# Half-width products for the super-tiles that carry only one layer

## The chip, the cores and the metric

The kernel runs on one core of one Trainium2 chip. The metric is the device time of one execution in microseconds (us), on that core. Every run below is of the state "fast" (none was over 1.5% above the fastest of its kernel). Engines are called PE (TensorE, matmul), PEld (its weight loads), DVE (VectorE), ACT (ScalarE), POOL (GpSimd) and SP (DMA issue).

## The reference, cut to what matters

```python
def _A_ref(x, mem0, Wq, Wk, Wv, Wo, seg_len):      # S=2048, Dm=448, H=16, Dh=256, M=8, seg_len=32
    mem = mem0
    for s in range(n_seg):                          # 64 segments, one after the other
        h = concatenate([mem, xs], axis=1)          # 8 memory rows + 32 tokens
        q, k, v = h @ Wq, h @ Wk, h @ Wv
        p = softmax(where(mask, q @ k * scale, -1e9))
        o = (p @ v) @ Wo
        mem = o[:, :M, :]                           # the memory rows feed the next segment
        outs.append(o[:, M:, :])

def _B_ref(x, W_gate, W_up, W_down):                # F=1792
    gate = relu-like(x @ W_gate);  return (gate * (x @ W_up)) @ W_down

x = x + _A_ref(layernorm(x), ...);  x = x + _B_ref(layernorm(x), ...)   # layer 0
x = x + _A_ref(layernorm(x), ...);  x = x + _B_ref(layernorm(x), ...)   # layer 1, same weights
```

The memory makes a recurrence over the 64 segments in each layer. Layer 1 can start segment s as soon as layer 0 has finished it.

## The kernel before

The two layers run as a pipeline, layer 1 four segments behind layer 0 (`LAG = 4`). One *step* t handles segment t of layer 0 and segment t-4 of layer 1; there are 68 steps. Two steps make a *super-tile* p (34 of them) of 128 rows: 64 tokens of layer 0 in rows 0 to 63 and 64 tokens of layer 1 in rows 64 to 127. Super-tiles 0 and 1 hold only layer 0, super-tiles 32 and 33 only layer 1; half of their rows are empty.

In each step the recurrence goes: score products of the segment (224 matmuls in `t_unit`), scores of the memory rows, softmax, transposes, the memory's value products, and the *memory value-sum* `un_mem` (56 products with 32 weight columns, four at once). Its result feeds the scores of the next step. Off this recurrence, but on TensorE too, lie the value-sum of the tokens (`un`), the layer norm (`ln_b`) and the gated MLP (`b_layer`), which run as filler while the recurrence waits for DVE and ACT. Their result is the input of layer 1 four steps later.

```python
    def un(self, p):                                        # value-sum: 56 products, 448 columns each
        for k in range(0, NO, 2):
            S.mm(lambda k=k: [MM(S.bO[:, 0:D], S.U[:, o, :], S.N[:, o, :], start=(o == 0), stop=(o == NO - 1)) for o in (k, k + 1)],
                 2 * S.pitch(D), uk[k // 16], S.ps(4))
        S.dve(lambda E: E.tensor_tensor(S.XB[:, p % 2, :], S.bO[:, 0:D], S.XA[:, p % 4, :], ALU.add), D, ...)

    def b_layer(self, p):
        for k in range(7):                                  # gate and up: 112 products, 128 columns each
            ...MM(R[w].b()[:, i * 128:i * 128 + 128], W[:, kt, fc * 128:fc * 128 + 128], S.xBT[:, kt, :], ...)
            S.act(... Relu ...);  S.dve(... tensor_tensor(hB, gT, up, ALU.mult) ...)
        for k in range(7):                                  # down: 14 products, 448 columns each
            S.mm(lambda k=k: [MM(S.bO[:, 0:D], S.hB[:, fc, :], S.Wd[:, fc, :], ...) for fc in (2 * k, 2 * k + 1)], ...)
        # then XA (input of layer 1, super-tile p + 2) and ys (output) = bO + XB
```

A scheduler in the file (`_Order`) sorts all these operations before the program is written: a greedy list scheduling by the longest path to the end. A change in one place can therefore reorder instructions elsewhere.

## Time and profile before

| | before |
|---|---|
| time | 1806.25 us median of 3 (1805.87 to 1811.62) |
| PE busy | 1733.2 of 1807.4 us (96%) |
| DVE, ACT busy | 59%, 40% |
| PE in the chain that ended last | 88% |
| one cycle of four steps in the middle | 103.09 us |

These lines are from the page of the profiled execution: the span, the busy time of each engine with its share and the number of instructions, and the shares of the chain of work that ended last.

```profile
span 1807.4 us, 67812 instructions
...
PE 1733.2 (96%) x30612; PEld 1247.2 (69%) x30612; DVE 1074.6 (59%) x3057; ACT 726.8 (40%) x2048; POOL 90.5 (5%) x155
...
PE 88%; DVE 7%; ACT 2%; SPq 1%; issue 1%; DMA 0%; DVEq 0%
```

PE is the limit. Its busy time is modelled, however, so the argument rests on the *starts* of matmuls in the trace. They give the pitch of a product: 189 ns for 448 columns, 56 ns for 128, 25 ns for 40.

The groups of instructions by line, engine and shape show the three kinds of product that the change touches (columns: engine, operation, output<-inputs, weight rows*columns, rows x columns of the moving operand, count | busy us, mean ns of one | idle before).

```profile
L127 PE MATMUL b<-Nw,big 128*128 128x448 bf16 x1928 | 414.7, 357 | 7.2 <-DVE big L683 5.2 <-issue 0.6
L127 PE MATMUL b<-xBT,big 128*128 128x128 bf16 x3808 | 233.5, 220 | 0.8 <-ACT xBT L682 0.7
...
L127 PE MATMUL b<-big,hB 128*128 128x448 bf16 x476 | 112.8, 354 | 0.0
```

The value-sum (`Nw,big`: 34 x 56 = 1904 products, the other 24 belong to the setup), gate/up (`xBT,big`, 34 x 112) and down (`big,hB`, 34 x 14) have one shape each: the four half-empty super-tiles pay the full width.

The end of the kernel is serial. The timeline of its last 28 us (start, duration, engine, line, operation, count, and the idle time before with what ended it):

```profile
1779.00 10.77 PE L127 MATMUL b<-Nw,big 128*128 128x448 bf16 x56
1789.81 0.62 DVE L953 TENSOR_TENSOR XB<-b,XA 128x448 bf16<-128x448 f32 x1 [10.10 <-PE b L127]
...
1792.64 0.40 PE L127 MATMUL b<-ident,xn 128*128 128x128 bf16 x4 [2.87 <-DVE xn L719]
...
1793.73 7.06 PE L127 MATMUL b<-xBT,big 128*128 128x128 bf16 x96 [0.69 <-ACT xBT L682]
...
1804.37 0.63 DVE L980 TENSOR_TENSOR ys<-b,XB 64x448 bf16<-64x448 f32 x1 [1.36 <-PE b L127]
```

The value-sum of super-tile 33 takes 10.8 us, the layer norm leaves PE waiting for 2.9 us and then 0.7 us, and gate, up and down take 10.6 us more.

These are stretches of the span with the busy time of each engine and the granted clock of PE (columns: stretch, length, busy us of PE, PEld, DVE, ACT, POOL with counts, PEclk, DMA share, GB/s): steps 1 to 5, steps 6 to 61, steps 62 to 65, and step 66 to the end.

```profile
93.54:211.18 117.64, 115.83 (x2095) 82.11 (x2095) 65.85 (x212) 37.80 (x108) 4.68 (x9) 0.98 0.01 3
211.18:1660.17 1448.99, 1407.34 (x25258) 1027.20 (x25257) 873.82 (x2436) 588.88 (x1652) 62.54 (x112) 1.00 0.02 5
1660.17:1754.57 94.40, 92.97 (x1750) 65.98 (x1749) 49.86 (x167) 38.26 (x113) 4.47 (x8) 1.00 0.02 4
1754.57:1807.39 52.82, 45.37 (x665) 32.49 (x664) 20.66 (x61) 13.58 (x39) 0.00 (x0) 0.97 0.02 4
```

The granted clock (the share of PE's full clock that the trace shows it was given) is not quite 1.00 at the two ends. The trace lists where: stretches of 3.4 us (once 6.8 us) at exactly half clock, at 36, 80 and 90 us, four times in the middle (at 503, 814, 1125 and 1435 us), and at 1793.5 us, in the gate/up products of the tail.

### The profile page before, as it was taken

To read this page: it belongs to the slowest core of one execution; us is meant where nothing else is said; L and a number is where in the kernel's file an instruction comes from. 1 tells how busy PE (TensorE), PEld (TensorE's weight loads), DVE (VectorE), ACT (ScalarE), POOL (GpSimd) and SP (SyncE) were. 2 spreads that over 40 slices of the span, in tenths; PEclk is the share of its full clock that TensorE was granted. 3 is DMA by queue.
4 is the path that set the end of the run, shared out by engine and by line. 5 is a ranking of instruction groups with operands and counts; after the bars stand their busy time and mean duration, and the time that the engine had idled before them with its cause. 6 is when DMAs were issued, how large, how long until landed. Compare 5 with 4: busy or idle time off the path is not lost.

```text
span 1807.4 us, 67812 instructions
## 1 busy us (share of the span) xinstructions
PE 1733.2 (96%) x30612; PEld 1247.2 (69%) x30612; DVE 1074.6 (59%) x3057; ACT 726.8 (40%) x2048; POOL 90.5 (5%) x155
## 2 busy tenths in 40 slices
PE   6899999999999999999999999999999999999998
PEld 2567667767766677677766776776667767766666
DVE  7645566665656566565655655565666656565553
ACT  5433433444343344434343444334334443434432
POOL 3000000000000000000000000000000000000000
PEclk9999999999999999999999999999999999999999
DMA  9700000000000000000000000000000000000000
GB/s 228 212 4 4 3 5 4 5 5 5 4 5 5 3 5 5 5 4 5 5 5 4 5 5 5 4 5 5 5 4 5 5 5 3 4 4 4 4 4 4
DMA packets 55760, 27.52 MB, mean 15 GB/s; under 512 B 44584, under 2 KB 54576, under 8 KB 55472
## 3 DMA queue, kind: packets, MB, share of 16 engines
q1 hardware_dynamic: 55120, 22.94, 5.2%
q8 instruction: 241, 3.95, 0.9%
q14 instruction: 47, 0.39, 0.1%
q10 hardware_dynamic: 352, 0.24, 0.1%
HBM read 10.33 MB, written 1.84 MB: 7 GB/s over the span
## 4 chain that ended last, share of the span: by engine, by line
PE 88%; DVE 7%; ACT 2%; SPq 1%; issue 1%; DMA 0%; DVEq 0%
PE b L127 88%; ACT big L682 2%; SPq L518 1%; DVE stat L712 1%; DVE big L683 1%; DVE TTs L683 1%; ACT hT L682 1%; DVE XB L953 1%; DVE xn L719 1%; DVE ys L980 1%; DVE XA L976 0%; DMA Nw<-in_A_Wq_dram 0%; DVE Es L841 0%; DVE stat L840 0%; DVE TTm L683 0%
## 5 line engine op out<-in xcount | busy, mean ns | idle before, releaser
L127 PEld LDWEIGHTS b<-hT,Mw 128*128 128x128 bf16 x15232 | 538.3, 100 | 26.3 <-DVE hT L683 12.0
L127 PE MATMUL b<-hT,Mw 128*128 128x80 bf16 (+1 forms) x15232 | 544.9, 199 | 5.7 <-DVE hT L683 3.9
L127 PE MATMUL b<-Nw,big 128*128 128x448 bf16 (+1 forms) x1936 | 415.8, 357 | 7.2 <-DVE big L683 5.2
L683 DVE CAST TTs<-b 128x320 bf16<-128x320 f32 (+5 forms) x572 | 261.2, 457 | 87.0 <-PE b L127 86.1
L127 PEld LDWEIGHTS b<-Nw,big 128*128 128x128 bf16 (+1 forms) x1936 | 172.2, 99 | 167.8 <-issue 22.3
L127 PE MATMUL b<-xBT,big 128*128 128x128 bf16 x3808 | 233.5, 220 | 0.8 <-ACT xBT L682 0.7
L127 PEld LDWEIGHTS b<-xBT,big 128*128 128x128 bf16 x3808 | 216.7, 98 | 3.2 <-ACT xBT L682 0.9
L683 DVE CAST TTm<-b 128x80 bf16<-128x80 f32 (+5 forms) x575 | 133.6, 232 | 125.9 <-PE b L127 95.0
L127 PE MATMUL b<-Nw,UTm 128*32 128x448 bf16 x3752 | 191.5, 355 | 0.6 <-ACT UTm L682 0.6
L683 DVE CAST big<-b 128x512 bf16<-128x512 f32 (+1 forms) x192 | 122.8, 661 | 104.4 <-PE b L127 103.4
L682 ACT ACTIVATE big<-b 128x512 bf16<-128x512 f32 (+1 forms) x320 | 152.6, 525 | 55.2 <-PE b L127 52.0
L127 PEld LDWEIGHTS b<-Nw,UTm 128*32 128x32 bf16 x3752 | 95.1, 97 | 88.7 <-issue 19.8
L683 POOL COPY hK<-xn 32x448 bf16<-32x448 bf16 x136 | 75.9, 558 | 1526.8 <-DVE xn L719 1520.5
L968 ACT ACTIVATE gT<-b 128x256 bf16<-128x256 f32 x238 | 91.5, 384 | 144.4 <-PE b L127 140.3
L682 ACT ACTIVATE TTs<-b 64x256 bf16<-64x256 f32 (+5 forms) x312 | 128.5, 412 | 31.2 <-PE b L127 26.6
L969 DVE TENSOR_TENSOR hB<-gT,b 128x256 bf16<-128x256 bf16 x238 | 99.5, 418 | 69.7 <-ACT gT L968 60.1
L682 ACT ACTIVATE TTm<-b 64x64 bf16<-64x64 f32 (+5 forms) x309 | 70.5, 228 | 143.4 <-PE b L127 136.8
L895 DVE TENSOR_TENSOR lo<-b,hi 128x448 bf16<-128x448 f32 x67 | 41.6, 620 | 127.3 <-ACT hi L894 127.3
L894 ACT ACTIVATE hi<-b 128x448 bf16<-128x448 f32 x67 | 36.5, 544 | 193.5 <-PE b L127 193.5
L127 PE MATMUL b<-big,hB 128*128 128x448 bf16 x476 | 112.8, 354 | 0.0
L682 ACT ACTIVATE hK<-b 8x448 bf16<-8x448 f32 x94 | 50.4, 536 | 124.3 <-PE b L127 122.9
L127 PE MATMUL b<-PTs,hK 40*128 40x512 bf16 (+1 forms) x640 | 86.7, 348 | 13.5 <-DVE XA L976 7.6
(96 smaller groups left out, 1392.5 us busy)
## 6 DMA issues: line engine op xcount, KB each, us to landing
big<-in_A_Wo_dram SPq DMA_DIRECT2D x3, 896.0 KB, 5.6
out_dram<-ys SPq DMA_DIRECT2D x32, 56.0 KB, 1.9
big<-in_B_W_down_dram SPq DMA_DIRECT2D x1, 1568.0 KB, 7.2
XA<-in_A_x_dram SPq DMA_DIRECT2D x28, 56.0 KB, 2.1
big<-in_B_W_up_dram SPq DMA_DIRECT2D x1, 1344.0 KB, 7.8
big<-in_B_W_gate_dram SPq DMA_DIRECT2D x1, 1344.0 KB, 8.8
Nw<-in_A_Wo_dram SPq DMA_DIRECT2D x1, 896.0 KB, 6.2
XA<-in_A_x_dram ACTq DMA_DIRECT2D x4, 56.0 KB, 4.3
```

Source lines behind the costliest of these rows:

```text
L127: ins = E.matmul(out, lhsT=lhsT, rhs=rhs, **kw)
L518: S.q.add("dma", ("sp",), {"sp": 3600.0}, lambda E: E.dma_start_transpose(out=st[w, q], in_=src[w][:, q * 1024:(q + 1) * 1024]), (), [(w, ...
L682: return E.activation(out(), src(), ACT.Copy)
L683: return E.tensor_copy(out(), src())
L712: S.dve(lambda E: E.bn_stats(st[:, so:so + 6], x), D, rd, [(key, 0)])
L719: S.dve(lambda E, a=a, b=b, src=src: E.tensor_scalar(S.xn[:, i, a:b], src, st[:, so + 6:so + 7], st[:, so + 8:so + 9], op0=ALU.subtract, o ...
L894: S.act(lambda E: E.activation(S.hi[:, :], b[:, 0:D], ACT.Copy), D, S.ps(6), [("hi",)])
L895: S.dve(lambda E: E.tensor_tensor(S.lo[:, :], b[:, 0:D], S.hi[:, :], ALU.subtract), D, S.ps(6) + [("hi",)], [("lo",)])
L953: S.dve(lambda E: E.tensor_tensor(S.XB[:, p % 2, :], S.bO[:, 0:D], S.XA[:, p % 4, :], ALU.add), D, S.ps(4) + [("XA", p % 4, 0), ("XA", p % ...
L968: S.act(lambda E, k=k, R=R: E.activation(S.gT[:, k % 2, 0:256], R[0].b()[:, 0:256], ACT.Relu), 256, R[0].res(), [("gT", k % 2)])
L969: S.dve(lambda E, k=k, R=R: E.tensor_tensor(S.hB[:, 2 * k:2 * k + 2, :].rearrange("p a b -> p (a b)"), S.gT[:, k % 2, 0:256], R[1].b()[:, ...
L980: S.dve(lambda E: E.tensor_tensor(S.ys[64:128, p % 2, :], S.bO[64:128, 0:D], S.XB[64:128, p % 2, :], ALU.add), D, S.ps(4, half=(1,)) + [(" ...
```

## The change

The intent: in the four super-tiles with one active layer, use the 64 rows that exist. The value-sum and down products then have only 64 weight columns, so two of them fit into the array side by side, one in each column half, each summing every second chunk; two adds on DVE join the two sums. Gate and up move 64 columns instead of 128.

```diff
+    def rows(p):
+        return slice(0, 64) if p < LAG // 2 else slice(64, 128) if p >= NSEG // 2 else slice(0, 128)
+    def halves(self, dst, base, base_keys, r, keys):
+        S.dve(lambda E: E.tensor_tensor(S.part[r, :], S.bO[0:64, 0:D], base, ALU.add), ...)
+        S.dve(lambda E: E.tensor_tensor(dst, S.bO[64:128, 0:D], S.part[r, :], ALU.add), ...)
     def un(self, p):
+        r = S.rows(p)
+        if r.stop - r.start == 128: ...as before...
+        else:
+            for k in range(0, NO, 4):
+                S.mm(lambda k=k: [MM(S.bO[64 * (o % 2):64 * (o % 2) + 64, 0:D], S.U[:, o, r], S.N[:, o, :], start=(o < 2), stop=(o >= NO - 2))
+                                  for o in range(k, k + 4)], 2 * S.pitch(D), uk[k // 16], S.ps(4), mode=6)
+            S.halves(S.XB[r, p % 2, :], S.XA[r, p % 4, :], ...)
     def b_layer(self, p):
-            fcs = (2 * k, 2 * k + 1)                        # two chunks of 128 columns a bank
+        w = r.stop - r.start;  m = 256 // w                 # or four of 64
...
-                return [MM(R[w].b()[:, i * 128:i * 128 + 128], ..., S.xBT[:, kt, :], ...)
+                return [MM(R[x].b()[:, i * w:i * w + w], ..., S.xBT[:, kt, r], ...)
...
-            S.mm(lambda k=k: [MM(S.bO[:, 0:D], S.hB[:, fc, :], S.Wd[:, fc, :], ...) for fc in (2 * k, 2 * k + 1)], ...)
+            S.mm(lambda k=k: [MM(S.bO[:, 0:D] if full else S.bO[64 * (fc % 2):64 * (fc % 2) + 64, 0:D], S.hB[:, fc, 0:w], ...)
+                              for fc in (2 * k, 2 * k + 1)], (2 if full else 1) * S.pitch(D), ..., mode=0 if full else 6)
```

(Cut: the joining adds of `b_layer`, a memset of the unused half of `XB`, and the `part` buffer.)

More of the change, by code (lines that the diff above doesn't have):

```diff
@@ L427, in alloc @@
         self.stat = self.sb("stat", [128, 96], F32)
+        self.part = self.sb("part", [128, D], F32)
         self.cvec = self.sb("cvec", [128, 2], F32)
@@ L559, in setup @@
         S.pool(lambda E: E.memset(S.Pm[:, :], 0.0), 128, (), [("Pm",)])
+        S.pool(lambda E: E.memset(S.XB[64:128, :, :], 0.0), 900, (), [("XB", 0), ("XB", 1)])
         S.pool(lambda E: E.memset(S.Ps[:, :, :], 0.0), 512, (), [("Ps",)])
@@ L945, in u_seg @@
                      R[l].res(), [("U", s, l, c)])
+    @staticmethod
+    def rows(p):
+        return slice(0, 64) if p < LAG // 2 else slice(64, 128) if p >= NSEG // 2 else slice(0, 128)
+    def halves(self, dst, base, base_keys, r, keys):
+        S = self
+        S.dve(lambda E: E.tensor_tensor(S.part[r, :], S.bO[0:64, 0:D], base, ALU.add), D, S.ps(4, half=(0,)) + base_keys, [("part",)])
+        S.dve(lambda E: E.tensor_tensor(dst, S.bO[64:128, 0:D], S.part[r, :], ALU.add), D, S.ps(4, half=(1,)) + [("part",)], keys)
     def un(self, p):
         S = self
+        r = S.rows(p)
         uk = [[("U", s, l, c) for s in range(2) for l in range(2)] for c in range(4)]
-        for k in range(0, NO, 2):
-            S.mm(lambda k=k: [MM(S.bO[:, 0:D], S.U[:, o, :], S.N[:, o, :], start=(o == 0), stop=(o == NO - 1)) for o in (k, k + 1)],
-                 2 * S.pitch(D), uk[k // 16], S.ps(4))
-        S.dve(lambda E: E.tensor_tensor(S.XB[:, p % 2, :], S.bO[:, 0:D], S.XA[:, p % 4, :], ALU.add), D,
-              S.ps(4) + [("XA", p % 4, 0), ("XA", p % 4, 1)], [("XB", p % 2)])
+        if r.stop - r.start == 128:
+            for k in range(0, NO, 2):
+                S.mm(lambda k=k: [MM(S.bO[:, 0:D], S.U[:, o, :], S.N[:, o, :], start=(o == 0), stop=(o == NO - 1)) for o in (k, k + 1)],
+                     2 * S.pitch(D), uk[k // 16], S.ps(4))
+            S.dve(lambda E: E.tensor_tensor(S.XB[:, p % 2, :], S.bO[:, 0:D], S.XA[:, p % 4, :], ALU.add), D,
+                  S.ps(4) + [("XA", p % 4, 0), ("XA", p % 4, 1)], [("XB", p % 2)])
+        else:
+            for k in range(0, NO, 4):
+                S.mm(lambda k=k: [MM(S.bO[64 * (o % 2):64 * (o % 2) + 64, 0:D], S.U[:, o, r], S.N[:, o, :], start=(o < 2), stop=(o >= NO - 2))
+                                  for o in range(k, k + 4)], 2 * S.pitch(D), uk[k // 16], S.ps(4), mode=6)
+            S.halves(S.XB[r, p % 2, :], S.XA[r, p % 4, :], [("XA", p % 4, r.start // 64)], r, [("XB", p % 2)])
         S.load_x(p + 4)
@@ L958, in b_layer @@
         S = self
-        for k in range(7):
-            fcs = (2 * k, 2 * k + 1)
-            R = [S.tile("R", 1) for w in range(2)]
-            def mms(fcs=fcs, R=R):
-                return [MM(R[w].b()[:, i * 128:i * 128 + 128], W[:, kt, fc * 128:fc * 128 + 128], S.xBT[:, kt, :], start=(kt == 0), stop=(kt == 3))
-                        for w, W in ((0, S.Wg), (1, S.Wu)) for i, fc in enumerate(fcs) for kt in range(4)]
-            S.mm(mms, 16 * S.pitch(128), [("xBT",)] + [(nm, x) for nm in ("Wg", "Wu") for x in "abz"], R[0].res() + R[1].res() + [("hB", k)])
-            S.act(lambda E, k=k, R=R: E.activation(S.gT[:, k % 2, 0:256], R[0].b()[:, 0:256], ACT.Relu), 256, R[0].res(), [("gT", k % 2)])
-            S.dve(lambda E, k=k, R=R: E.tensor_tensor(S.hB[:, 2 * k:2 * k + 2, :].rearrange("p a b -> p (a b)"), S.gT[:, k % 2, 0:256],
-                                                      R[1].b()[:, 0:256], ALU.mult), 256, R[1].res() + [("gT", k % 2)], [("hB", k)])
@@ L971, in b_layer, with mms @@
-        for k in range(7):
-            S.mm(lambda k=k: [MM(S.bO[:, 0:D], S.hB[:, fc, :], S.Wd[:, fc, :], start=(fc == 0), stop=(fc == NFC - 1)) for fc in (2 * k, 2 * k + 1)],
-                 2 * S.pitch(D), [("hB", k), ("Wd",)], S.ps(4))
+        r = S.rows(p)
+        w = r.stop - r.start
+        m = 256 // w
+        for k in range(-(-NFC // m)):
+            fcs = range(m * k, min(m * k + m, NFC))
+            n = len(fcs) * w
+            R = [S.tile("R", 1) for _ in range(2)]
+            hk = [("hB", f // 2) for f in fcs[::2]]
+            def mms(fcs=fcs, R=R):
+                return [MM(R[x].b()[:, i * w:i * w + w], W[:, kt, fc * 128:fc * 128 + 128], S.xBT[:, kt, r], start=(kt == 0), stop=(kt == 3))
+                        for x, W in ((0, S.Wg), (1, S.Wu)) for i, fc in enumerate(fcs) for kt in range(4)]
+            S.mm(mms, 8 * len(fcs) * S.pitch(w), [("xBT",)] + [(nm, x) for nm in ("Wg", "Wu") for x in "abz"],
+                 R[0].res() + R[1].res() + hk)
+            S.act(lambda E, k=k, R=R, n=n: E.activation(S.gT[:, k % 2, 0:n], R[0].b()[:, 0:n], ACT.Relu), n, R[0].res(), [("gT", k % 2)])
+            S.dve(lambda E, k=k, R=R, n=n, fcs=fcs: E.tensor_tensor(
+                S.hB[:, fcs[0]:fcs[-1] + 1, 0:w], S.gT[:, k % 2, 0:n].rearrange("p (a b) -> p a b", b=w),
+                R[1].b()[:, 0:n].rearrange("p (a b) -> p a b", b=w), ALU.mult), n, R[1].res() + [("gT", k % 2)], hk)
@@ L974, in b_layer @@
+        full = w == 128
+        for k in range(7):
+            S.mm(lambda k=k: [MM(S.bO[:, 0:D] if full else S.bO[64 * (fc % 2):64 * (fc % 2) + 64, 0:D], S.hB[:, fc, 0:w], S.Wd[:, fc, :],
+                                 start=(fc < (1 if full else 2)), stop=(fc >= NFC - (1 if full else 2))) for fc in (2 * k, 2 * k + 1)],
+                 (2 if full else 1) * S.pitch(D), [("hB", k), ("Wd",)], S.ps(4), mode=0 if full else 6)
+        xb = [("XB", p % 2)]
         if p < NSEG // 2:
             q = p + LAG // 2
-            S.dve(lambda E: E.tensor_tensor(S.XA[64:128, q % 4, :], S.bO[0:64, 0:D], S.XB[0:64, p % 2, :], ALU.add), D,
-                  S.ps(4, half=(0,)) + [("XB", p % 2)], [("XA", q % 4, 1)])
+            if full:
+                S.dve(lambda E: E.tensor_tensor(S.XA[64:128, q % 4, :], S.bO[0:64, 0:D], S.XB[0:64, p % 2, :], ALU.add), D,
+                      S.ps(4, half=(0,)) + xb, [("XA", q % 4, 1)])
+            else:
+                S.halves(S.XA[64:128, q % 4, :], S.XB[0:64, p % 2, :], xb, r, [("XA", q % 4, 1)])
@@ L978, in b_layer @@
         if p >= LAG // 2:
             q = p - LAG // 2
-            S.dve(lambda E: E.tensor_tensor(S.ys[64:128, p % 2, :], S.bO[64:128, 0:D], S.XB[64:128, p % 2, :], ALU.add), D,
-                  S.ps(4, half=(1,)) + [("XB", p % 2)], [("ys", p % 2)])
+            if full:
+                S.dve(lambda E: E.tensor_tensor(S.ys[64:128, p % 2, :], S.bO[64:128, 0:D], S.XB[64:128, p % 2, :], ALU.add), D,
+                      S.ps(4, half=(1,)) + xb, [("ys", p % 2)])
+            else:
+                S.halves(S.ys[64:128, p % 2, :], S.XB[64:128, p % 2, :], xb, r, [("ys", p % 2)])
```

## The prediction

> **What bounds it now.** TensorE. On the page PE is busy 1733.2 of 1807.4 us (96%) and the chain of waits is 88% PE. VectorE is 59% busy. The stretches between two memory value-sums (one per step, timeline) repeat in a cycle of four steps: 25.7, 25.65, 26.9, 24.8 us, each within 0.8 to 1.8 us of its matmul work (pitch times count). The two first and two last super-tiles carry one layer but pay full width in their value-sum (56 matmuls N=448), gate/up (112, N=128) and down (14, N=448) products.
>
> **Costs.** From matmul starts in the trace: 448 columns 189 ns, 128 columns 56 ns, 40 columns 25 ns. The Trainium skill, "TensorE: Matmul & The Clock Gate", Back-to-back issue gap, gives N/2.4 + 2.5 ns with a floor of about 25 ns; the trace agrees, so I estimate 29 ns at N=64. Two column-half products of 448 columns already run in the setup (weights folded, 64-column outputs): the two start 3 ns apart and pairs follow every 189 ns, so halves really are two for one. A switch of tiling costs: first product after it 85 to 96 ns late, the next pair 210 instead of 189, and 96 ns on leaving. ("TensorEngine Tiling (Array Packing)", Key Properties: a mode switch drains; the trace shows it.) About 0.2 us per excursion.
>
> Per super-tile: value-sum 10.6 to 5.3 us, gate/up 6.3 to 3.3, down 2.65 to 1.3: 9.6 us, 38 us for four. The instruction order of the new kernel leaves steps 6 to 61 with the same matmuls; it adds about 30 tiling switches, some 3 us. One more VectorE add of 448 columns (0.63 us) per value-sum and per down product. The Pool memset is off the chain.
>
> **How much counts** (estimates, step by step):
> - Steps 1 to 5: now 20.5, 22.8, 23.6, 25.7, 25.1 us. Matmul work falls by 3.6, 5.9, 2.0, 5.7, 1.8. Steps 1 and 2 then hit the recurrence (memory value-sum, hi, lo, transposes, 224 score products, softmax, transposes, copy: about 17 us for one layer), switches take some: net about -16.
> - Steps 62 to 65: work falls by 5.3, but in the new order the last full down product moves behind the memory value-sum, and the next layer norm and score products wait for it, so about -2.5.
> - Step 67 with super-tile 32's GLU: -4.
> - Tail, all serial, 1779.0 to 1805.0: value-sum -5.3, gate/up -3.0, down -1.2, two extra adds +1.3: -8.
>
> Sum about -30 us: 1776 us, 1.7% less. Just under the 2% line, because four of 34 super-tiles change and about a fifth of the 38 us is given back to switches, extra adds and the recurrence.
>
> **Range** 1768 to 1785. Faster by over 2% 0.15, same 0.84, slower 0.01.
>
> **What would show it.** The timeline: column-half pairs at 189 ns, N=64 at about 29 ns, tail from the last value-sum's start to the end about 18 us instead of 26; steps 1 to 5 together about 101 us instead of 118; the four-step cycle still 103.1 us; more VectorE and fewer PE shares in the chain at the ends.
>
> **What would make it wrong.** Column-half weight loads not hidden (pair pitch over 189 ns); N=64 held by its weight loads; the recurrence longer than 17 us, or hidden so well that nearly all 38 us are gained; other half-clock windows: the clock now halves for 3.4 us about every 310 us, costing 1.4 us each, and their number may change by one or two, above all in the tail, where PE waits through the layer norm.

## More of the kernel before

The experiments ran in four rounds on four chips, with the kernel before run again in each: its 34 executions there lay between 1805.2 and 1812.1 us (0.4%), its medians between 1807.6 and 1808.4. So a few microseconds out of 1800 can be told apart with several runs, and differences of one or two between kernels of different rounds can't.

## The result

The changed kernel took 1783.91 us (median of 4, 1782.1 to 1784.83), the kernel before 1807.05 us in the same rounds. The ratio is 0.9866, 95% interval 0.9847 to 0.9885. (Ratios here are the mean time of one kernel's fast runs over that of the other's of the same rounds, so not quite the ratio of the medians quoted beside them.) That is 1.3% faster, within 2%. The forecast was 1776 us and 1.7%; the range 1768 to 1785 holds the result, near its upper edge.

The two profiled executions differ by 27.1 us (1807.4 and 1780.3 us), the medians by 23.1. Both numbers are true; why they differ is part of the answer below.

The page of the changed kernel, the lines that answer to those of before:

```profile
span 1780.3 us, 67770 instructions
...
PE 1700.7 (96%) x30612; PEld 1226.7 (69%) x30612; DVE 1073.2 (60%) x3058; ACT 720.6 (40%) x2031; POOL 91.0 (5%) x156
...
PE 75%; DVE 6%; ACT 2%; issue 1%; DVEq 0%
```

The chain accounts for only part of the span this time (its shares sum to about 85%), so its PE share can't be set against the 88%. The shapes:

```profile
L127 PE MATMUL b<-Nw,big 128*128 128x448 bf16 x1704 | 368.8, 358 | 7.8 <-DVE big L685 5.6 <-issue 0.7
...
L127 PE MATMUL b<-Nw,big 128*64 128x448 bf16 x232 | 26.1, 357 | 0.4 <-DVE ys L958 0.4
...
L127 PE MATMUL b<-xBT,big 128*128 128x128 bf16 x3360 | 204.0, 219 | 0.0
...
L127 PE MATMUL b<-xBT,big 128*128 128x64 bf16 x448 | 15.6, 199 | 0.7 <-ACT xBT L684 0.7
...
L127 PE MATMUL b<-big,hB 128*128 128x448 bf16 x420 | 99.7, 354 | 0.0
...
L127 PE MATMUL b<-big,hB 128*64 128x448 bf16 x56 | 7.6, 363 | 0.0
```

4 x 56 value-sum products, 4 x 112 gate/up products and 4 x 14 down products moved to the narrow shapes, as intended. The mean time of a single column-half product is still about 360 ns, like that of a full-width product, although these follow each other every 189 ns; only the starts show the gain. From the trace (start in us, gap to the matmul before in ns):

```
1732.132  +109   Nw,big  64 weight columns, 448   <- first after 40-column products (pitch 25)
1732.136    +4   Nw,big  64 weight columns, 448
1732.346  +210   Nw,big                           <- the next pair, 21 late
1732.349    +3   Nw,big
1732.634  +285   hT,TTm  128 weight columns, 40   <- back to full width (189 + 96)
...
1733.235  +186   Nw,big                           <- inside a run: a pair every 189
1753.528   +29   xBT,big 128 weight columns, 64
```

Two things forecast from the setup's products hold: column halves are truly two for one, and each switch of tiling costs about 90 ns. The Trainium skill says in "TensorEngine Tiling (Array Packing)", Key Properties, that changing the tiling mode drains TensorE; here is the size of it.

The tail, timeline of the changed kernel:

```profile
1760.26 5.49 PE L127 MATMUL b<-Nw,big 128*64 128x448 bf16 x56 [0.42 <-DVE ys L958]
1765.79 0.62 DVE L957 TENSOR_TENSOR part<-b,XA 64x448 f32<-64x448 f32 x1 [4.95 <-PE b L127]
1766.44 0.63 DVE L958 TENSOR_TENSOR XB<-b,part 64x448 bf16<-64x448 f32 x1
...
1769.27 0.40 PE L127 MATMUL b<-ident,xn 128*128 128x128 bf16 x4 [3.52 <-DVE xn L721]
...
1770.36 4.78 PE L127 MATMUL b<-xBT,big 128*128 128x64 bf16 x112 [0.69 <-ACT xBT L684]
...
1775.07 1.52 PE L127 MATMUL b<-big,hB 128*64 128x448 bf16 x14
...
1777.28 0.63 DVE L958 TENSOR_TENSOR ys<-b,part 64x448 bf16<-64x448 f32 x1
```

From the start of the value-sum to the end it is 17.7 us instead of 26.0 (forecast: 18). The value-sum is halved; one more add of 0.63 us stands before the layer norm and one at the very end.

The stretches that answer to those of before:

```profile
92.84:196.72 103.88, 100.46 (x2096) 71.29 (x2095) 64.79 (x207) 35.39 (x106) 4.66 (x9) 0.98 0.01 4
196.72:1646.05 1449.33, 1407.44 (x25257) 1027.29 (x25257) 873.40 (x2436) 588.40 (x1652) 62.31 (x112) 1.00 0.02 5
1646.05:1737.91 91.86, 88.95 (x1744) 64.14 (x1743) 50.28 (x171) 37.32 (x109) 4.45 (x8) 0.98 0.02 4
1737.91:1780.30 42.39, 32.58 (x672) 24.55 (x670) 19.15 (x57) 12.40 (x35) 0.00 (x0) 0.92 0.02 5
```

Steps 1 to 5 fall from 117.6 to 103.9 us, steps 62 to 65 from 94.4 to 91.9, the rest from 52.8 to 42.4. Steps 6 to 61 did not change (1449.0 and 1449.3): the order of instructions there is the same. The clock at the end fell from 0.97 to 0.92.

To see where the 38 us of removed work went, I divide PE's time by the starts of its matmuls: to each matmul belongs its pitch (*work*); what the gap to the next is longer goes to a *tiling switch* (up to 100 ns, where the weight shape changes), to *half clock* (inside such a stretch, up to one pitch), or to *waiting*. For the two ends together (steps 0 to 5 and 62 to the end), in us:

| | before | after | difference |
|---|---|---|---|
| work | 249.5 | 211.4 | -38.1 |
| tiling switches | 9.7 | 12.7 | +3.0 (32 more) |
| half clock | 5.1 | 6.8 | +1.7 |
| waiting | 19.9 | 25.5 | +5.6 |
| length of the ends | 284.3 | 256.5 | -27.8 |

Work and switches came as forecast. The waiting and the half clock are what the experiments are about.

### The profile page after: what moved, and what is told of

Its sections match the earlier page's. It is cut to its first block, busy times and chain, and to the rows that moved or that the text cites. A ratio compares the mean times of both kernels' runs of the same rounds, so it can differ in the third digit from the quotient of the medians.

```text
span 1780.3 us, 67770 instructions
## 1 busy us (share of the span) xinstructions
PE 1700.7 (96%) x30612; PEld 1226.7 (69%) x30612; DVE 1073.2 (60%) x3058; ACT 720.6 (40%) x2031; POOL 91.0 (5%) x156
## 4 chain that ended last, share of the span: by engine, by line
PE 75%; DVE 6%; ACT 2%; issue 1%; DVEq 0%
PE b L127 75%; ACT big L684 1%; DVE big L685 1%; DVE stat L714 1%; DVE TTs L685 1%; DVE xn L721 1%; ACT hT L684 1%; DVE ys L1015 1%; DVE XA L1008 1%; DVE XB L968 0%; DVE Es L843 0%; DVE stat L842 0%; DVE TTm L685 0%; DVE hT L685 0%; DVE part L957 0%
## 5 line engine op out<-in xcount | busy, mean ns | idle before, releaser
L127 PEld LDWEIGHTS b<-hT,Mw 128*128 128x128 bf16 x15232 | 539.8, 100 | 25.3 <-DVE hT L685 11.2
L127 PE MATMUL b<-Nw,big 128*128 128x448 bf16 (+1 forms) x1936 | 394.9, 358 | 8.2 <-DVE big L685 5.6
L127 PEld LDWEIGHTS b<-Nw,big 128*128 128x128 bf16 (+1 forms) x1936 | 163.7, 100 | 157.1 <-issue 21.5
L127 PE MATMUL b<-xBT,big 128*128 128x128 bf16 (+1 forms) x3808 | 219.6, 217 | 0.7 <-ACT xBT L684 0.7
L127 PEld LDWEIGHTS b<-xBT,big 128*128 128x128 bf16 x3808 | 204.7, 98 | 2.4 <-ACT xBT L684 0.9
L685 DVE CAST big<-b 128x512 bf16<-128x512 f32 (+1 forms) x190 | 121.3, 659 | 103.9 <-PE b L127 102.8
L995 ACT ACTIVATE gT<-b 128x256 bf16<-128x256 f32 x226 | 86.4, 382 | 128.8 <-PE b L127 124.1
L684 ACT ACTIVATE TTm<-b 64x64 bf16<-64x64 f32 (+4 forms) x304 | 69.4, 228 | 159.4 <-PE b L127 152.5
L996 DVE TENSOR_TENSOR hB<-gT,b 128x256 bf16<-128x256 bf16 x226 | 93.6, 415 | 64.8 <-ACT gT L995 54.0
L127 PE MATMUL b<-big,hB 128*128 128x448 bf16 (+1 forms) x476 | 107.3, 355 | 0.0
L127 PE MATMUL b<-PTs,hK 40*128 40x512 bf16 (+1 forms) x640 | 86.4, 348 | 13.3 <-DVE XA L1008 7.1
```

What stands on the lines that cost most here:

```text
L127: ins = E.matmul(out, lhsT=lhsT, rhs=rhs, **kw)
L684: return E.activation(out(), src(), ACT.Copy)
L685: return E.tensor_copy(out(), src())
L995: S.act(lambda E, k=k, R=R, n=n: E.activation(S.gT[:, k % 2, 0:n], R[0].b()[:, 0:n], ACT.Relu), n, R[0].res(), [("gT", k % 2)])
L996: S.dve(lambda E, k=k, R=R, n=n, fcs=fcs: E.tensor_tensor(S.hB[:, fcs[0]:fcs[-1] + 1, 0:w], S.gT[:, k % 2, 0:n].rearrange("p (a b) -> p a ...
```

## The experiments

My theory (A throughout): each part of the change is worth its work on PE, less about 0.1 us per added switch, less what turns into waits for the recurrence and for the chain through the layer norms. The rivals: that the switches are hidden; that the recurrence already sets the steps at the ends; that PE's clock, not its work, takes the gain back.

All experiments start from the changed kernel, except where the text says otherwise. "Ends" means the sum over steps 0 to 5 and 62 to the end in the profiled execution, the difference to the 284.3 us of before.

### The parts alone

**Value-sum alone**: `b_layer` works on 128 rows again.

```diff
     def b_layer(self, p):
-        r = S.rows(p)
+        r = slice(0, 128)
```

> Only the value-sum of the four single-layer super-tiles runs in column halves; gate, up and down products stay 128 rows wide. Theory A (each part is worth its TensorE work, less about 0.1 us per added tiling switch, less what falls into waits for the recurrence): work falls by 21.2 us, 20 more switches cost 2.0 us, one extra add of 0.65 us in the tail, so 15 to 19 us faster than before. Rival B (the value-sum is the part that gives its gain back, to switches and the recurrence): under 10 us. In the trace: pairs still follow every 189 ns.

Measured: 1801.35 us against 1807.64 (ratio 0.9963). Theory A missed by more than half; the number is rival B's (under 10 us), but not all of its reason. The ends are only 8.2 us shorter: work -21.2, switches +2.0, waiting +6.2, half clock +4.8. The trace says where. In step 3 and in the tail, PE now waits for a layer norm with nothing left to fill the time, and the clock halves right after it. From the timeline of this kernel:

```profile
139.93 0.40 PE L127 MATMUL b<-ident,xn 128*128 128x128 bf16 x4 [2.19 <-DVE xn L721]
...
140.80 9.78 PE L127 MATMUL b<-hT,Mw 128*128 128x80 bf16 x224
```

```profile
1774.93 5.49 PE L127 MATMUL b<-Nw,big 128*64 128x448 bf16 x56
1783.95 0.61 PE L127 MATMUL b<-ident,xn 128*128 128x128 bf16 x4 [3.53 <-DVE xn L721]
1785.25 7.91 PE L127 MATMUL b<-xBT,big 128*128 128x128 bf16 x96 [0.69 <-ACT xBT L684]
```

The 224 score products at 140.80 took 9.8 us instead of about 8.2, and 96 gate/up products in the tail 7.9 us instead of 7.1.

**Gate and up alone**: `un` on 128 rows, the down product on all 128 rows of `hB`.

```diff
     def un(self, p):
-        r = S.rows(p)
+        r = slice(0, 128)
...
-        full = w == 128
+        full = True                    # and hB keeps each token's own column: S.hB[:, fcs, r]
```

(Cut: a memset of `hB` on POOL in the setup, for the columns that nothing writes.)

> Only gate and up products are cut to 64 rows. Work falls by 12.0 us and nearly no switch is added (5). Theory A: 9 to 12 us faster. Rival B (in the first super-tiles the freed time turns into waits for the recurrence, as the products are only filler there): 6 us or less, with the gain only in steps 66 and after.

Measured: 1797.03 against 1807.64 us (0.9943), 10.6 us faster. The ends are 12.0 us shorter, 6.0 at each, which is all of the work that was taken away; the profiled execution had five half-clock stretches in steps 6 to 61, that of before four. Theory A holds, and rival B, which had the gain at the end only, is out. Five more switches (0.5 us by the starts), no extra add, no more waiting in sum: the simplest part of the change is the one that pays in full.

**Down alone**: `un` and gate/up on 128 rows, `halves` only after the down product.

```diff
-        full = w == 128
+        h = S.rows(p);  full = h.stop - h.start == 128
...
-        S.hB[:, fc, 0:w]
+        S.hB[:, fc, h]
```

> Only the down product runs in column halves (gate and up 128 rows wide, value-sum full). Work falls by 5.3 us, 3 more switches, one extra add per super-tile of which the one at the very end lies on the chain (0.65 us). Theory A: 3 to 5 us faster. Rival B (extra add and switches eat it): 0 to 2 us.

Measured: 1804.49 against 1807.64 us (0.9986, interval 0.9968 to 1.0004). Inconclusive by time: it lies between the two. By the ends, rival B: 0.4 us shorter, nearly all of the 5.3 us of work came back as 3.7 us of waiting, 0.8 us of half clock and 0.3 us of switches. The profiled execution was 5.6 us shorter all the same, because it happened to have no half-clock stretch in steps 6 to 61, where that of before had four.

**Value-sum and gate/up together**, down at full width.

```diff
-        full = w == 128
+        full = True                    # S.hB[:, fcs, r] and memset as in "gate and up alone"; un stays changed
```

> Value-sum in column halves and gate/up at 64 rows, the down product left at full width. The single parts took 8.2 us (value-sum), 12.0 us (gate/up) and 0.4 us (down) off the steps at the two ends by their traces, 20.6 us in sum, the whole change 27.8. Theory A (the parts share their waits: once value-sum and gate/up are both short, the last down product of a layer is through before the memory value-sum that used to push the layer norm back, so value-sum and gate/up together already give more than their sum): 23 to 27 us off the ends, ratio to before about 0.987. Rival B (the surplus is in the down product): 19 to 21 us off the ends, ratio about 0.989.

Measured: 1786.47 against 1808.42 us (0.9886), the ends 22.2 us shorter. Theory A's idea, that the value-sum and gate/up share their waits, fell: 22.2 is about the sum of the two (8.2 + 12.0). The surplus of the whole over its parts (27.8 against 20.6) comes with the down product, which is worth 0.4 us alone and 5.6 us on top of the other two, as rival B had it. (By time it is less clear: 2.6 us by the medians, 3.6 by the ratios, whose intervals overlap.) This kernel has half-clock stretches in steps 3 and 4 (2.9 us) that the whole change doesn't have, and 1.1 us more waiting in step 4. Why the short down product avoids them was not isolated; that it stands right before the layer norm that these steps wait for is only an argument.

**The last two super-tiles alone.**

```diff
-        return slice(0, 64) if p < LAG // 2 else slice(64, 128) if p >= NSEG // 2 else slice(0, 128)
+        return slice(64, 128) if p >= NSEG // 2 else slice(0, 128)
```

> The whole change, but in the two last super-tiles alone. Theory A from the step table of the changed kernel's trace: steps 0 to 61 as before, steps 62 to the end 11 to 14 us shorter, so 11 to 14 us faster than before by the trace, the rest of the whole change's gain (about 14 us) being in the first two. Rival B (the ends interact through the phase of the four-step cycle or the clock windows): the two halves of the change do not add up to the whole within 3 us.

Measured: 1791.76 against 1807.64 us (0.9916), steps 62 to the end 134.2 us. In the whole change they take 134.25 us, before 147.2. So, by the steps, the two ends don't touch each other: 13 us are earned at the end, the other 14.9 us in steps 0 to 5. By time this kernel is 15.9 us faster, more than its ends show; its profiled execution had one half-clock stretch in steps 6 to 61 where that of before had four. The first two super-tiles alone were not run.

### Is a switch really paid?

One product of 8 columns at full width goes into the middle of every value-sum piece, which makes 112 more switches.

```diff
             for k in range(0, NO, 4):
+                T = S.tile("R", 1)
...
-                                  for o in range(k, k + 4)], ...
+                                  for o in (k, k + 1)] +
+                     [MM(T.b()[:, 0:8], S.ident[:, :], S.ident[:, 0:8], start=True, stop=True)] +
+                     [... for o in (k + 2, k + 3)], ...
```

> The changed kernel with one 8-column product of full width put into the middle of each value-sum piece of the four single-layer super-tiles: 56 extra excursions out of the column-half mode (112 more switches), 1.4 us of work. Theory A (an excursion costs about 0.2 us of TensorE time, and TensorE is the limit where the pieces run): 8 to 13 us slower than the changed kernel. Rival B (switches are hidden in waits and cost nothing): at most 3 us slower. Pair pitch in the trace stays 189 ns inside a piece.

Measured: 1796.12 us (1790.94 to 1802.09), 12.2 us slower than the changed kernel. The profiled execution was the slowest of the four, its ends 19.0 us longer: the accounting gives 10.2 us to the 112 added switches, 91 ns each, 4.4 us to half clock, 1.4 us to the added products and some 3 us to waiting. Theory A holds. A switch is paid in full, and the 32 that the change adds cost about 3 us.

### Does the recurrence already set these steps?

The value-sums of super-tiles 0 and 32 are cut to 8 of 56 products. The result is wrong (the comparison with the reference still passed, presumably because what these products add is small beside the residual; so that comparison says little of these products, in the changed kernel too).

```diff
-            for k in range(0, NO, 4):
+            for k in ((0, NO - 4) if p in (0, NSEG // 2) else range(0, NO, 4)):
```

> Wrong result on purpose: the value-sums of super-tiles 0 and 32 are cut to 8 of 56 products, which takes another 9.1 us of TensorE work (4.5 us in steps 1 to 3, 4.5 us in steps 65 and 66). Theory A (with the change, the recurrence and the chain through the layer norms already set the time of the steps in which these products are filler): at most 4 us faster than the changed kernel, the freed work turning up as waits. Rival B (TensorE work still sets those steps): 7 to 9 us faster.

Measured: 1775.72 us (ratio to before 0.9819, against 0.9866 of the changed kernel), 8.2 us faster, within rival B. The profiled execution shows less: its ends are 5.9 us shorter (2.1 us went to half clock and 1.9 to waiting), and it had three half-clock stretches in steps 6 to 61 where the changed kernel had four. Either way my theory fell here: of another 9.1 us of work, more than half came off the time. Step 2 went from 17.6 to 16.0 us, below the 17 us that I had taken for the length of the recurrence; steps 3, 65 and 66 and the tail got shorter too, step 1 did not (18.3 to 19.3 us, with 1.5 us more waiting). So the recurrence is not the limit of step 2, and PE's work still sets most of these steps.

### Are the waits at the end waits for something else, and do they cost the clock?

Useless products (448 columns against an identity, into a bank that is free) are put in front of the instructions that PE waits to start. They are inserted after the scheduler has run, so the order of everything else is that of the changed kernel.

```diff
         self.q.run()
+        self.fill()                     # inserts n products before the named operation, into the bank it will write
         self.q.emit()
+    FILL = {'pt65': 5, 'la33': 2, 'tu67': 4, 'lb33': 17, 'g33': 2}
```

> The changed kernel, same order, with 30 useless products (448 columns, 5.7 us of TensorE work at full clock) put into the gaps in which TensorE waits in the last three steps: 5 and 2 before the two transposes in step 65, 4 before the scores of step 67, 17 and 2 around the last layer norm. Theory A (these gaps are waits for serial chains on VectorE and ScalarE, and the half-clock windows at the end follow from them): no slower, and 1.5 to 4 us faster than the changed kernel as the half-clock windows in steps 65, 66 and the tail go away. Rival B (TensorE work sets the end): 4 to 6 us slower.

Measured: 1779.86 us (1774.4 to 1783.51), 4.1 us faster than the changed kernel although PE does 5.7 us more work. By time alone this is weak: the ratio is 0.9845 (0.9828 to 0.9863), an interval that overlaps that of the changed kernel, and the runs scatter with their clocks (0.990 to 0.995). The steps decide. Steps 62 to the end fell from 134.25 to 131.3 us, their half-clock loss from 3.1 us to nothing. Theory A holds, rival B is out: these gaps are waits for serial work on DVE and ACT, and the idleness itself costs clock. The lines of the same places in the changed kernel, timeline of PE:

```profile
1723.22 0.40 PE L127 MATMUL b<-ident,Ps 128*128 128x128 bf16 x4 [1.12 <-DVE Ps L847]
...
1724.52 0.40 PE L127 MATMUL b<-ident,xn 128*128 128x128 bf16 x4 [0.53 <-DVE xn L721]
```

and with the filling of both ends and of the middle (the kernel with the fill at both ends and in the middle, further below), where the 17 products stand in the gap of the last layer norm and the 112 gate/up products after it take 3.4 instead of 4.8 us:

```profile
1755.60 3.39 PE L127 MATMUL b<-Nw,ident 128*128 128x448 bf16 x17
1759.20 0.40 PE L127 MATMUL b<-ident,xn 128*128 128x128 bf16 x4 [0.21 <-DVE xn L739]
1759.43 0.54 PE L127 MATMUL b<-Nw,ident 128*128 128x448 bf16 x2
1760.28 3.44 PE L127 MATMUL b<-xBT,big 128*128 128x64 bf16 x112 [0.31 <-ACT xBT L702]
```

**Both ends filled**: `'mt0': 5, 'pm1': 6` are added, products in two gaps of steps 0 and 1.

> As the one before, with 11 more useless products in the gaps of steps 0 and 1 (before the transposes of the memory and before the softmax transpose). Theory A: the two half-clock windows at about 80 and 91 us go away or shrink, another 1.5 to 4 us faster than with the end alone, 3 to 7 us faster than the changed kernel in all. Rival B: the windows stay (they follow from the setup) and it is 0 to 2 us slower than with the end alone.

Measured: 1776.48 us, 7.4 us faster than the changed kernel and 3.4 faster than with the end alone, about as theory A had it. Steps 0 and 1 lose nothing to half clock any more (3.7 us in the changed kernel), and step 1 takes 16.2 instead of 18.3 us.

**The middle filled too.** The half-clock stretches in steps 6 to 61 all follow the same place, 5 to 8.5 us into every fourth step (9, 13, ... 61), where PE waits three times for 0.2 to 0.5 us. In the changed kernel, step 21, right before its half-clock stretch at 592.3 us:

```profile
590.11 0.61 PE L127 MATMUL b<-PTs,hK 40*128 40x512 bf16 x4 [0.50 <-DVE XA L1008]
...
591.42 0.39 PE L127 MATMUL b<-PTs,hK 40*128 40x512 bf16 x2 [0.21 <-ACT big L684]
592.18 4.13 PE L127 MATMUL b<-Nw,big 128*128 128x448 bf16 x12 [0.37 <-DVE big L685]
```

The 12 value-sum products at 592.18 took 4.1 us instead of 2.4. The stretches that begin with step 21 and with its half clock show the granted clock (PEclk, the third figure from the end):

```profile
583.82:592.30 8.48, 7.39 (x94) 3.09 (x94) 5.16 (x11) 4.81 (x12) 0.00 (x0) 1.00 0.03 9
592.30:595.70 3.40, 3.40 (x10) 1.32 (x9) 1.80 (x5) 2.11 (x5) 1.14 (x3) 0.50 0.00 0
```

Two useless products go before the first of these waits and two before the last.

```diff
+    FILL = {..., 'mt9': 2, 'mt13': 2, ... 'mt61': 2, 'un4': 2, 'un6': 2, ... 'un30': 2}
```

> The changed kernel with useless products in the waits of both ends and in every fourth steady step. Theory A: no half-clock window left between 40 us and the end, 1769 to 1773 us, 2 to 7 us faster than with the ends alone and 11 to 15 us faster than the changed kernel; the difference to the kernel before with the same filling (both without windows) is 23 to 27 us. Rival B: no faster than with the ends alone.

Measured: 1770.9 us, four runs within 1 us (1770.65 to 1771.58), against 1808.42: ratio 0.9794, interval 0.9781 to 0.9807. It beats both kernels. Its profiled execution has a single half-clock stretch, at 35 us in the setup, and all four runs have a granted clock of 0.999. The same place in step 21, where the 12 products now take 2.4 us:

```profile
589.12 0.55 PE L127 MATMUL b<-Nw,ident 128*128 128x448 bf16 x2
589.56 2.44 PE L127 MATMUL b<-Nw,big 128*128 128x448 bf16 x12
```

**The same filling in the kernel before** (15 and 2 products around the last layer norm, 5 and 6 in steps 0 and 1, the same places in the middle; none in step 65 or before the scores of step 67).

> The kernel before, with useless products in its waits: 5 and 6 in steps 0 and 1, 15 and 2 around the last layer norm, 2 and 2 in every fourth step (9 to 61) where the half-clock window falls. Theory A (the half-clock windows follow from these waits): windows at 80, 90 and in the steady steps are gone, 5 to 12 us faster than before, and the spread of its runs shrinks to about 2 us. Rival B (windows come whatever TensorE does): 0 to 3 us slower.

Measured: 1800.56 us (1799.03 to 1801.57) against 1808.42: ratio 0.9957. Windows of steps 1 to 5 and of step 66 to the end in this kernel:

```profile
93.95:209.84 115.89, 114.07 (x2094) 81.56 (x2093) 66.05 (x212) 38.02 (x109) 4.67 (x9) 1.00 0.01 3
...
1747.84:1799.15 51.31, 47.08 (x682) 32.55 (x681) 20.66 (x61) 13.62 (x39) 0.00 (x0) 1.00 0.02 4
```

The same two in the changed kernel with all its filling:

```profile
92.38:194.05 101.67, 98.24 (x2095) 70.62 (x2094) 64.87 (x207) 35.70 (x106) 4.68 (x9) 1.00 0.02 4
...
1728.76:1768.89 40.13, 34.77 (x695) 24.37 (x693) 19.16 (x57) 12.32 (x35) 0.00 (x0) 1.00 0.02 6
```

The clock is 1.00 where it was 0.98 and 0.97 in the kernel before, 0.98 and 0.92 in the changed one. So the filling wins back 7.9 us of half clock in the kernel before, and 13.0 us in the changed kernel (1783.91 to 1770.9; by the ratios to before, 0.9866 and 0.9794, the same). These are net of what the useless products cost where they don't fit a gap, and one half-clock stretch, at 86 us in step 0, is left in the filled kernel before (1.1 us). With both filled, the change is worth 1800.56 - 1770.9 = 29.7 us, more than the 23 to 27 expected here, and within a microsecond of the 30 us that the prediction had summed.

### The extra adds

In the filled version, the first of the two adds is cut to 8 columns; the order on every engine stays the same. The result is wrong.

```diff
-        S.dve(lambda E: E.tensor_tensor(S.part[r, :], S.bO[0:64, 0:D], base, ALU.add), ...)
-        S.dve(lambda E: E.tensor_tensor(dst, S.bO[64:128, 0:D], S.part[r, :], ALU.add), ...)
+        S.dve(lambda E: E.tensor_tensor(S.part[r, 0:8], S.bO[0:64, 0:8], base[:, 0:8], ALU.add), ...)
+        S.dve(lambda E: E.tensor_tensor(dst, S.bO[64:128, 0:D], base, ALU.add), ...)
```

> Wrong result on purpose: the filled version (no half-clock windows, runs within 1 us of each other), same order on every engine, with the first of the two adds after each column-half product cut from 448 columns to 8, which should take about 0.45 us off each of the eight. Theory A (the extra add counts where a serial chain waits for it, and that is the two in the tail and, in part, the one before super-tile 32's layer norm; the others are under TensorE work): 0.8 to 1.8 us faster than the filled version. Rival B (each of the eight lies on the chain): 3 us or more.

Measured: 1768.23 us, 2.7 us faster than the filled version by the medians and 3.1 by the ratios of the two rounds (0.9777 and 0.9794), so the time alone does not part the two expectations. By steps, 1.6 us of it lie in step 66 and the tail, 0.4 us in step 2 and 0.3 us in steps 4 and 5; step 3 of this execution had a half-clock stretch and can't be compared. So, as far as the steps show, the adds count mostly in step 66 and the tail, as theory A had it, with a little more elsewhere than it allowed.

## Why the prediction was right, and where it was off

The time lay in the range and the call "within 2%" was right. Point by point:

- *TensorE is the limit, and the removed work is 38 us*: right. 38.1 us of work went, at 189 ns a pair and 29 ns for 64 columns. That PE's work still sets most of the steps at the ends was shown by taking more of it away.
- *About 30 more switches, some 3 us*: right. 32, 3.0 us; 91 ns each where 112 were added.
- *Steps 6 to 61 unchanged, cycle of 103.1 us*: right (103.08).
- *Steps 62 to 65: -2.5*: right (-2.5). *Tail 18 instead of 26 us*: right (17.7).
- *Steps 1 to 5: -16 because "Steps 1 and 2 then hit the recurrence"*: they gave 13.8, and the reason was wrong. Cutting more work shortened step 2 to 16.0 us. Of 19.0 us of work, switches took 2.1 (22 more), waits 2.6 and half clock 0.5 us. With both kernels filled it is still 14.2, so the clock is not what is missing here.
- *Step 67 with super-tile 32's GLU (its gate, up and down products): -4*: it gave 2.1 (from the memory value-sum of step 66 to the last value-sum, 24.4 to 22.35 us). This stretch has the extra adds and a half-clock stretch of its own.
- *Half-clock windows "may change by one or two"*: named, but left out of the sum. This is the term that was mis-sized. The prediction put them at zero net. They cost 7.9 us in the kernel before and 13.0 us after, by the filled pair: a net 5.1 us. The clocks say much the same without any filling: the share of the clock that was not granted, times the span, an estimate of the time lost, is 13.3 us on average over 34 runs of the kernel before (clock 0.991 to 0.996) and 19.6 us over the four of the changed kernel (0.989 each). With 5.1, -30 becomes -25; the result was -23 to -24 (0.9866 of 1807.05 is 24.2 us less). Shorter work does not only uncover waits, the waits then lower the clock of what comes after: that was shown at the ends. But in the two profiled executions only 1.7 us of the 5.1 lie there, and steps 6 to 61 have four stretches in both. The rest would have to lie in other executions of the kernel before that had fewer stretches in the middle, as its higher clocks suggest; why the change should alter that, with the same instructions and waits there, is not shown.
- That the filled kernels differ by 29.7 us and the prediction summed 30 is in part luck: by steps the filled pair gives -1.6 in step 0 (forecast 0; 1.1 of it is the stretch that was left), -14.2 in steps 1 to 5 (-16), -3.4 in steps 62 to 65 (-2.5) and -11.2 from step 66 on (-12).
- The half-clock stretches also make executions of one kernel differ. The profiled executions of these kernels had between none and five in steps 6 to 61, at about 1.45 us each, with the same order of instructions there; the filled version, with none, repeats within 1 us, where the four runs of the down product alone spread over 5.5. The profiled execution of the kernel before was 2 to 3 us above its medians (1809.19 us, at 0.991 the lowest clock for it), that of the changed kernel 1.8 us below its own (1782.1 us): hence 27.1 us by the profiles and 23.1 by the medians. The first fits the clock; the second is too small to show in clocks noted to 0.001.

What stays open: why the down product is worth 0.4 us alone and 5.6 us with the rest, and by what measure the hardware decides to halve the clock. One thing more is in the traces: in all 14 of them every change of the clock comes a whole multiple of 3.413 us after the last (307.2 us is 90 of them), and this grid lies differently against step 0 in each, by up to 3.3 us. That its place decides which of several like waits is followed by a half-clock stretch, and so how many an execution has, is likely and was not tested.

## What to carry to other kernels

Here a product with half the weight columns really cost half in column halves (a pair every 189 ns), and one with half the moving columns cost about half (29 instead of 56 ns) with hardly a switch, no join and no new wait; try the second kind first. Where work is removed from a stretch that fills waits, count what the waits then do to PE's clock: look for half-clock stretches before and after, in several executions, and test with useless products in the gaps, placed after scheduling so that the order stays. Such filling was worth 8 us in one kernel and 13 us in the other, and it made a measurement of small differences possible at all.

## What the Trainium skill lacked or had wrong

- "TensorE: Matmul & The Clock Gate", the table "Why this matters for your kernels", asks for no PE-idle gaps over about 3 us. That was not enough here. The half-clock stretches of 3.4 us in steps 6 to 61 (the page's window length, 3413 ns, agrees) followed 3.4 us in which PE was idle for 0.9 to 1.1 us in all and hardly more than 0.5 us at a time; the same waits in ten of the 14 cycles of the kernel before were not followed by one. The page also has a kernel whose clock swings because PE idles briefly and often, but gives no size for that. Four products of 189 ns in each such place removed all of them in steps 6 to 61.
- The same page, Back-to-back issue gap, gives about 81 ns per matmul at 128 columns and 131 ns at 512 as the sustained rate of weight-load and matmul pairs. This trace, with a weight load for every matmul, runs 128 columns at 56 ns, 448 at 189 ns and 40 at 25 ns, which is the page's other formula, N/2.4 + 2.5 with a floor of about 25, that it calls the gap of an isolated matmul.
- "TensorEngine Tiling (Array Packing)", Key Properties, says that a mode switch drains, without a size. It was 91 ns a switch over 112 of them, about 0.2 us for an excursion.
- The same page, Gotcha 2: Feature Incompatibilities, says that column tiling and fast weight load exclude each other, without a cost. With 448 moving columns no cost showed here: pairs follow every 189 ns, the pitch of a single full-width product.
